# A fused adaLN / spectral mixer / MLP forward and backward kernel: loads of the first stage in a stated order, modulation rows dealt out singly, eight early blocks, and the first MLP block placed ahead of the last tile's products

## The chip, the core and the metric

The kernel runs on one core of a Trainium2 chip as a single launch. The metric is the device time of one execution in microseconds (us), from runs without the profiler; three runs of the kernel before are known, and their median is the number to beat. Separately, one execution was taken by the hardware profiler; every trace row in this document comes from such an execution. TensorE (PE) does the matrix products, VectorE (DVE) and ScalarE (ACT) do the elementwise work and empty PSUM, GpSimd (POOL) makes index tables and issues indirect transfers and many stores, and SyncE (SP) issues most loads. SP and POOL each issue in their own fixed order: an issue that waits holds up every issue behind it on that engine.

## The reference: what is computed

The reference is the forward pass of one block and its gradient (a VJP) for one sequence of 2048 tokens with 1024 features. Cut to what matters:

```python
def _A_ref(x, w_r, w_i):                  # spectral mixer
    X = rfft2(x) ; X = X * (w_r + 1j * w_i)
    return irfft2(X)
def _B_ref(x, w1, b1, w2, b2):            # MLP, 1024 -> 3584 -> 1024
    return gelu(layernorm(x) @ w1 + b1) @ w2 + b2
sa, ca, ga, sb, cb, gb = split6(silu(c) @ w_mod)
h = layernorm(x) * (1 + ca) + sa ;  x = x + ga * _A_ref(h)
h = layernorm(x) * (1 + cb) + sb ;  x = x + gb * _B_ref(h)
out, vjp = jax.vjp(...) ;  returns out and vjp(grad_out) for nine inputs
```

Arrays are bf16. The six rows `sa` to `gb` are rows 0 to 5 of the modulation.

## The kernel before

**Stages.** Both transforms are written as products with cosine and sine matrices. PE goes through these stages: modulation rows and a transposition of `grad_out`; the product `gb*grad_out` times `w2` transposed, called `pp` and stored as `d_ph`, which the gradient of the GELU needs later; the forward spectral mixer; more of `pp`; the MLP forward in four token blocks (`z_block` for the first matrix, `bo_pass` for the second); and from about 700 us on the backward stages and weight gradients, which no line of the change touches.

**How the order comes about.** The program is traced in Python; a scheduler then puts the instructions of each engine into a fixed order, earlier traced work first where it can run, later traced work in the gaps it expects. `tc.issue_after(ins)` keeps the instructions of a block behind `ins` on the engine of `ins` alone, and `behind(a, b)` does so for one pair. `ordered()` means: behind the last matrix product that was noted in `last_pe`. A tile with a tag takes over the memory of an earlier tile with that tag once that one's last reader is done.

**First stage (L264 to L395).** `mod_block(r, h)` (L272) makes half `h` of modulation row `r`: eight products of a 1 MB weight block `wblk` into a PSUM buffer of the two in `ps_s`, and one copy out of it. The blocks go round a ring of three tiles (`mod_tile`, L264), so that a load waits for the products three blocks before. Rows 1 and 5 come first. `load_tok` (L141) loads a quarter of the tokens: one 512 KB transfer from SP and two indirect ones from POOL. `load_go` (L349) loads a 1 MB quarter of `grad_out`; L381 to L395 transpose the four quarters on PE, four 128x128 products for each of 32 PSUM tiles (four buffers, `ps_f`), and DVE and ACT alternately scale each tile by `gb_col` into `gBoT0` to `gBoT3`. `gb_col` comes from both halves of row 5. `load_w2t(fg)` (L340) loads two chunks (256 rows) of `w2` with a transposing DMA into one of two halves of `wt`.

**The early `pp` chunks (L802 to L827).** `ph_part(fc, js)` makes chunk `fc` (of 28) for the token quarters `js`: eight products for each quarter into a `ps_f` buffer, and a copy out on ACT or DVE; I call one such quarter a part. `PH_EARLY = 6` chunks are traced ahead of the layer norms and folds that feed the spectral mixer (L829 to L846); the scheduler pulls later chunks forward as filler. Behind the products of chunk 3 stand three modulation blocks in a row, and behind chunk 5 three more (rows 2, 3 and 4). Row 0 and the table generator `gen_mats` are traced ahead of all `pp`.

**The late chunks and the first MLP block (L882 to L1055).** `load_w2t(fc // 2)` is issued as the two chunks before in the same half of `wt` are done. `load_w1` puts the seven 1 MB tiles of `w1` on SP behind given `w2` loads: two at chunk 22, one at chunk 24, four at chunk 26. The last four chunks get only quarters 0 and 1 at first. Then comes a list, `plan` (L1030): MLP block (0, 0), quarters 2 and 3 of chunks 24 to 27, MLP blocks (0, 1) and so on. `z_block` (L918) loads `n3T` (the normed tokens, transposed), makes four groups of eight products into `ps_s` and `ps_d`, and copies them to `zb`, a tile over the memory of `gBoT0` and `gBoT1`.

Of the kernel before, what the change touches and what calls it, by code (L numbers as in the profile page):

```python
# [10 lines left out]
FP32 = mybir.dt.float32  # L11
BF16 = mybir.dt.bfloat16
# [5 lines left out]
P = 128  # L18
# [17 lines left out]
def kernel(  # L36
# [104 lines left out]
    def load_tok(t4, src, i, eng=None):  # L141
        s3 = tok_flat(src)
        ins = (eng or nc.sync).dma_start(out=tok_plain(t4, i), in_=tok_rows(s3, i, 0, D))
# [120 lines left out]
    def mod_tile():  # L264
        wring[0] += 1
        return reg.tile([P, NDC, KH], BF16, name="wblk", tag=PXT[3 + wring[0] % 3])

    def mod_load(r, h, wblk, eng):
        cb = 2 * r + h
        eng.dma_start(out=wblk, in_=w_mod[:, cb * KH:(cb + 1) * KH].rearrange("(j p) n -> p j n", p=P))  # L270

    def mod_block(r, h, wblk=None):  # L272
        if wblk is None:
# [66 lines left out]
    def load_w2t(fg):  # L340
        w2t_in[0] = nc.sync.dma_start_transpose(out=wt[:, fg % 2], in_=B_w2[fg * 256:(fg + 1) * 256, :])
        w2ts.append(w2t_in[0])
# [4 lines left out]
           fbuf[:, 2], fbuf[:, 3]]  # L347

    def load_go(j):  # L349
        nc.sync.dma_start(out=gos[j], in_=go_f[j * BW:(j + 1) * BW, :].rearrange("(a p) d -> p a d", p=P))  # L350

    wm = {}

    def mod_get(r, h):
        wm[r, h] = mod_tile()
        mod_load(r, h, wm[r, h][:], nc.sync)

    mod_get(1, 0)
    load_tok(x4s[0], A_x, 0)
    mod_get(1, 1)  # L360
    mod_get(5, 0)
    for h in range(2):
        mod_block(1, h, wm[1, h][:])
    mod_get(5, 1)
    load_go(0)
    load_w2t(0)
    load_go(1)
    load_tok(x4s[1], A_x, 1)
    load_go(2)
    load_go(3)  # L370
    for h in range(2):
        mod_block(5, h, wm[5, h][:])
    load_tok(x4s[2], A_x, 2)
    load_tok(x4s[3], A_x, 3)
    load_w2t(1)
    pc = ps_d("pc")
    for cch in range(NDC):
        nc.tensor.matmul(pc[:, cch:cch + 1], lhsT=gb_row[0:1, cch * P:(cch + 1) * P], rhs=ones_bf[0:1, 0:1], start=True, stop=True)
# [398 lines left out]
        nc.vector.tensor_copy(out=out, in_=in_)  # L777


    for h in range(2):  # L780
        mod_block(0, h)
    gen_mats()
    gb2s = small.tile([P, NDC], FP32, tag="u_rt", bufs=1)
    nc.vector.reduce_sum(out=gb2s[:], in_=gu[:, 0:4, :].rearrange("p j c -> p c j"), axis=AX.X)
    gb2_bf = small.tile([P, NDC], BF16, tag="gc_bf", bufs=1)
    nc.vector.tensor_copy(out=gb2_bf[:], in_=gb2s[:])
    to_rows(gb2r, gb2_bf[:], NDC, ident[:])
    nc.gpsimd.dma_start(out=out_7.rearrange("(c p) -> c p", p=P), in_=gb2r)
    nc.gpsimd.dma_start(out=b1r, in_=B_b1.rearrange("(f p) -> f p", p=P))
    to_cols(b1_col[:], b1r, NFC, ident[:])  # L790
    nc.vector.tensor_scalar(out=sar[:, 0], in0=sar[:, 0], scalar1=8.0, scalar2=None, op0=ALU.mult)
    fold_d(saf.rearrange("p (c d) -> p c d", c=1), sar[:, 0], sar[:, 1])


    pho = reg.tile([P, 3, 4, BW], BF16, name="pho", tag="ot")
    phs = [pho[:, k] for k in range(3)] + [reg.tile([P, 4, BW], BF16, name="phr", tag="ph")[:]]
    last_pe = [None]

    def ordered():
# [118 lines left out]
    def z_block(b, g0, g1):  # L918
        n3T = n3Ts[b % 2]
        if g0 == 0:  # L920
            with tc.issue_after(w2ts[11].ins) if b == 0 else ExitStack():
                n3_in = nc.sync.dma_start_transpose(out=n3T[:], in_=d_n3[b * BW:(b + 1) * BW, :])
            if b == 0:
                for ins in w1_in[:2]:
                    behind(ins, n3_in)
        for g in range(g0, g1):
            n = b * 7 + g
            zb, av, bv, sg, ph = gts[n % 2]
            hh = hh_slots[n % 11]
            with tc.issue_after(w2t_in[0].ins) if n < 2 else ExitStack():  # L930
                nc.sync.dma_start(out=ph, in_=d_ph_v[:, g * 4:(g + 1) * 4, b * BW:(b + 1) * BW])
            for k in range(4):
                fc = g * 4 + k
                pz = (ps_s, ps_d)[k % 2]("pz")
                for cch in range(NDC):
                    with ordered():
                        last_pe[0] = nc.tensor.matmul(pz[:], lhsT=w1s[g][:, cch, k * P:(k + 1) * P], rhs=n3T[:, cch, :],  # L937
                                                      start=(cch == 0), stop=(cch == NDC - 1))
                with tc.high_priority():
                    z_in = nc.scalar.activation(out=zb[:, k, :], in_=pz[:], func=ACT.Identity, bias=b1_col[:, fc:fc + 1], scale=1.0)  # L940
            if n == 3:
                behind(n3_sqrt, z_in)
            elif n == 4:
                for ins in n3_norm:
                    behind(ins, z_in)
            with after_ev():
                nc.scalar.activation(out=av, in_=zb, func=ACT.Square)  # L947
            nc.vector.tensor_scalar(out=av, in0=av, scalar1=GC, scalar2=1.0, op0=ALU.mult, op1=ALU.add)
            tt(bv, av, zb, ALU.mult)
            with after_ev():  # L950
                nc.scalar.activation(out=sg, in_=bv, func=ACT.Sigmoid, scale=2.0 * GK)  # L951
            with after_ev():
                nc.scalar.activation(out=bv, in_=bv, func=ACT.Sigmoid, scale=-2.0 * GK)  # L953
            nc.vector.tensor_scalar(out=av, in0=av, scalar1=6.0 * GK, scalar2=-4.0 * GK, op0=ALU.mult, op1=ALU.add)
            tt(hh, sg, zb, ALU.mult)
            nc.gpsimd.dma_start(out=d_hh_v[:, g * 4:(g + 1) * 4, b * BW:(b + 1) * BW], in_=hh)
            tt(av, av, bv, ALU.mult)
            tt(av, av, hh, ALU.mult)
            tt(av, av, sg, ALU.add)
            if b < 2:  # L960
                tt(ph, ph, av, ALU.mult)
            for k in range(4 if b >= 2 else 0):
# [588 lines left out]
```

## Time and profile before

| what | value |
|---|---|
| runs without profiler | 1415.97, 1416.61, 1421.49 us; median 1416.61 us |
| the profiled execution, its own time | 1419.22 us |
| its span, first to last instruction | 1417.4 us |
| mean granted TensorE clock | 0.990 |
| DMA | 333.22 MB, mean 235 GB/s |

The profiled execution spends 1.8 us outside its span. Busy shares are read with care: a product is counted from its start to a modelled end, so "busy" PE rows hold some pipeline, and a few per cent of the product records are missing. In timeline rows the first column is the start, the second the length of a merged run of instructions, `x` the recorded number, and the bracket the idle time of that engine just before, with what ended it. In rows by stretches, each engine has its busy time and in brackets the number of instructions; then come the granted TensorE clock, the share of DMA time, and GB/s.

### The profile page before, as it was taken

The numbers are of one execution on the slowest core, as the hardware profiler recorded it, in microseconds if no ns is written. First come the engines' busy times: TensorE is split into PE (matmuls) and PEld (weight loads), VectorE is DVE, ScalarE is ACT, GpSimd is POOL, SyncE is SP. The second block draws the span as 40 slices with busy tenths as digits, with TensorE's granted clock in tenths as the row PEclk, the third lists the DMA queues.
The fourth block names the chain that finished last, engine by engine and source line by source line (L and its number), as shares of the span: only waits on it lengthen the run. The fifth ranks groups of instructions, "written<-read, shape, count | busy, mean of one in ns | idle before, by whom it ended". The sixth has DMA issues, their size and how long they took to land. (4 is left out here: it accounts for less than half of the span.)

```text
span 1417.4 us, 18569 instructions
## 1 busy us (share of the span) xinstructions
PE 1367.5 (96%) x6839; PEld 663.0 (47%) x6963; DVE 1071.1 (76%) x1503; ACT 745.6 (53%) x1063; POOL 377.1 (27%) x479
## 2 busy tenths in 40 slices
PE   5999999999999999999999999999999999999998
PEld 2545675444444444444444444344544565444443
DVE  5898889987698877886520788999488659898642
ACT  4775667667887765666315583343623445343211
POOL 5500623201112122212210011011367432322332
PEclk8899999999999999999999999999999999999999
DMA  9972647899688776687999399996699997666993
GB/s 330 304 226 72 181 137 226 261 277 348 239 235 267 231 252 233 200 275 232 292 287 233 115 271 319 210 298 193 191 279 281 242 242 207 189 180 182 288 261 118
DMA packets 356689, 333.22 MB, mean 235 GB/s; under 512 B 207578, under 2 KB 297200, under 8 KB 356470
## 3 DMA queue, kind: packets, MB, share of 16 engines
q1 hardware_dynamic: 319110, 205.61, 55.1%
q0 software_dynamic: 37488, 126.42, 25.7%
q8 instruction: 54, 0.88, 0.3%
q14 instruction: 37, 0.30, 0.1%
HBM read 166.77 MB, written 115.92 MB: 199 GB/s over the span
## 5 line engine op out<-in xcount | busy, mean ns | idle before, releaser
L808 PE MATMUL pp<-gBoT,wt 128*128 128x512 bf16 x874 | 196.3, 381 | 4.0 <-DMA wt<-in_B_w_dram 2.8
L1094 PE MATMUL pg<-w1T,gzr 128*128 128x512 bf16 x877 | 195.0, 379 | 3.7 <-ACT gn3b L1109 1.7
L1445 PE MATMUL gw1acc<-gzh,n3n 128*128 128x512 bf16 x877 | 194.1, 379 | 1.0
L1094 PEld LDWEIGHTS <-gzr 128*128 128x128 bf16 x896 | 86.4, 98 | 110.8 <-issue 7.9
L808 PEld LDWEIGHTS <-wt 128*128 128x128 bf16 x896 | 87.6, 98 | 107.5 <-DMA wt<-in_B_w_dram 3.3
L937 PEld LDWEIGHTS <-w 128*128 128x128 bf16 x896 | 87.1, 98 | 107.4 <-issue 2.7
L1445 PEld LDWEIGHTS <-n3n 128*128 128x128 bf16 x896 | 87.2, 98 | 105.2 <-issue 1.3
L937 PE MATMUL pz<-n3Ta,w 128*128 128x512 bf16 x439 | 98.2, 379 | 1.8 <-ACT gt L940 1.3
L937 PE MATMUL pz<-n3Tb,w 128*128 128x512 bf16 x436 | 98.0, 379 | 0.7 <-issue 0.2
L940 ACT ACTIVATE gt<-pz,b_col 128x512 bf16<-128x512 f32 x112 | 73.5, 684 | 38.1 <-PE pz L937 37.6
L994 PEld LDWEIGHTS <-hhA 128*128 128x128 bf16 x608 | 58.9, 98 | 73.4 <-issue 3.0
L1227 PE MATMUL gw2acc<-gB,hhsA 128*128 128x512 bf16 x406 | 91.2, 379 | 0.5
L1449 ACT CAST gwo<-gw1acc 128x512 bf16<-128x512 f32 x49 | 28.5, 582 | 111.0 <-PE gw1acc L1445 103.2
L194 DVE TENSOR_TENSOR gt<-gt,gt 128x2048 bf16<-128x2048 bf16 x56 | 68.5, 1224 | 20.6 <-ACT gt L953 19.4
L951 ACT ACTIVATE gt<-gt 128x2048 bf16<-128x2048 bf16 x28 | 53.5, 1910 | 55.1 <-DVE gt L194 55.1
L194 DVE TENSOR_TENSOR ct<-ct 128x2048 bf16<-128x2048 bf16 x68 | 80.8, 1217 | 1.4 <-DMA d_n<-ct 0.5
L1234 ACT CAST gwo<-gw2acc 128x512 bf16<-128x512 f32 x46 | 26.7, 582 | 101.0 <-PE gw2acc L1227 83.2
L1227 PEld LDWEIGHTS <-hhsA 128*128 128x128 bf16 x416 | 40.6, 98 | 47.9
L947 ACT ACTIVATE gt<-gt 128x2048 bf16<-128x2048 bf16 x28 | 53.5, 1910 | 1.7 <-DVE w2sA L194 1.0
L1450 POOL DMA_DIRECT2D out_dram<-gwo x56 | 30.7, 549 | 88.6 <-ACT gwo L1449 66.2
L953 ACT ACTIVATE gt<-gt 128x2048 bf16<-128x2048 bf16 x28 | 53.4, 1908 | 0.4
L814 ACT CAST pho<-pp 128x512 bf16<-128x512 f32 x59 | 33.5, 582 | 32.4 <-PE pp L808 31.9
(346 smaller groups left out, 2544.5 us busy)
## 6 DMA issues: line engine op xcount, KB each, us to landing
gzr<-d_gz SPq DMA_DIRECT2D x28, 512.0 KB, 6.4
wblk<-in_w_mod_dram SPq DMA_DIRECT2D x12, 1024.0 KB, 8.8
out_dram<-otl POOLq DMA_DIRECT2D x48, 256.0 KB, 4.5
out_dram<-gwo POOLq DMA_DIRECT2D x96, 128.0 KB, 4.2
d_ph<-pho POOLq DMA_DIRECT2D x21, 512.0 KB, 5.6
d_hh<-hhA POOLq DMA_DIRECT2D x19, 512.0 KB, 5.0
w<-in_B_w_dram SPq DMA_DIRECT2D x7, 1024.0 KB, 11.7
hhC<-d_ph SPq DMA_DIRECT2D x14, 512.0 KB, 9.5
```

The source lines that it names most:

```text
L194: return nc.vector.tensor_tensor(out=out, in0=a, in1=b, op=op)
L808: last_pe[0] = nc.tensor.matmul(pp[:], lhsT=wt[:, fg % 2, cch, k * P:(k + 1) * P], rhs=gBoT[j][:, cch, :], start=(cch == 0), stop=(cch == ...
L814: nc.any.tensor_copy(out=ov, in_=pv)
L937: last_pe[0] = nc.tensor.matmul(pz[:], lhsT=w1s[g][:, cch, k * P:(k + 1) * P], rhs=n3T[:, cch, :], start=(cch == 0), stop=(cch == NDC - 1))
L940: z_in = nc.scalar.activation(out=zb[:, k, :], in_=pz[:], func=ACT.Identity, bias=b1_col[:, fc:fc + 1], scale=1.0)
L947: nc.scalar.activation(out=av, in_=zb, func=ACT.Square)
L951: nc.scalar.activation(out=sg, in_=bv, func=ACT.Sigmoid, scale=2.0 * GK)
L953: nc.scalar.activation(out=bv, in_=bv, func=ACT.Sigmoid, scale=-2.0 * GK)
L994: last_pe[0] = nc.tensor.matmul(pbs[i][:], lhsT=hh[:, k, i * P:(i + 1) * P], rhs=wp[:, k, :], start=False, stop=(g == 6 and k == 3))
L1094: last_pg[0] = nc.tensor.matmul(pgs[i][:], lhsT=gzs[b, g][:, k, i * P:(i + 1) * P], rhs=w1Ts[g][:, k, h * KH:(h + 1) * KH], start=(g == 0 ...
L1227: nc.tensor.matmul(acc[:], lhsT=hh_of(fc)[:, t, :], rhs=gBs[t // 4][:, t % 4, h * KH:(h + 1) * KH], start=(t == 0), stop=(t == NT - 1))
L1445: nc.tensor.matmul(acc[:], lhsT=n3ns[t // 4][:, t % 4, cch * P:(cch + 1) * P], rhs=gz2[t // 8][:, t % 8, :], start=(t == 0), stop=(t == NT ...
```

## The change

Four things are edited.

1. The loads of the first stage are chained on SP with `start_load`: row 1 half 0, token quarter 0, row 1 half 1, row 5 half 0, `grad_out` quarter 0; then row 5 half 1, `grad_out` quarters 1, 2 and 3, token quarter 1, `w2` tile 0, token quarters 2 and 3, `w2` tile 1. Only SP instructions are chained; the indirect loads on POOL are not.
2. Chunks 0 and 1 of `pp` are traced ahead of row 0 and `gen_mats`, and row 0's products stand behind chunk 1's.
3. `PH_EARLY` is 8. The six late modulation blocks are put singly behind given parts (`MOD_AT`), two or three parts apart.
4. Chunks 26 and 27, quarters 0 and 1, move behind MLP block (0, 0) in `plan` (kind "q"). `w1` tiles are loaded one at chunk 22, one at chunk 24, five at chunk 26, and the last five stand behind the first load of `d_ph`.

```diff
     def mod_load(r, h, wblk, eng):
...
+        return eng.dma_start(out=wblk, in_=w_mod[:, cb * KH:(cb + 1) * KH].rearrange("(j p) n -> p j n", p=P))
...
-    mod_get(1, 0)
-    load_tok(x4s[0], A_x, 0)
-    mod_get(1, 1)
-    mod_get(5, 0)
+    last_ld = [None]
+
+    def start_load(what, *a):
+        with tc.issue_after(last_ld[0].ins) if last_ld[0] else ExitStack():
+            if what == "w":
+                wm[a] = mod_tile()
+                last_ld[0] = mod_load(*a, wm[a][:], nc.sync)
+            elif what == "t":
+                load_w2t(*a)
+                last_ld[0] = w2t_in[0]
+            elif what == "g":
+                last_ld[0] = load_go(*a)
+            else:
+                last_ld[0] = load_tok(x4s[a[0]], A_x, a[0])
+
+    for what in (("w", 1, 0), ("x", 0), ("w", 1, 1), ("w", 5, 0), ("g", 0)):
+        start_load(*what)
     for h in range(2):
         mod_block(1, h, wm[1, h][:])
-    mod_get(5, 1)
-    load_go(0)
-    load_w2t(0)
-    load_go(1)
-    load_tok(x4s[1], A_x, 1)
-    load_go(2)
-    load_go(3)
+    for what in (("w", 5, 1), ("g", 1), ("g", 2), ("g", 3), ("x", 1), ("t", 0), ("x", 2), ("x", 3), ("t", 1)):
+        start_load(*what)
     for h in range(2):
         mod_block(5, h, wm[5, h][:])
-    load_tok(x4s[2], A_x, 2)
-    load_tok(x4s[3], A_x, 3)
-    load_w2t(1)
...
-    phs = [pho[:, k] for k in range(3)] + [reg.tile([P, 4, BW], BF16, name="phr", tag="ph")[:]]
+    phs = [pho[:, k] for k in range(3)]
...
-    PH_EARLY = 6
+    for fc in range(2):
+        ph_part(fc, (0, 1, 2, 3))
+    with ordered():
+        for h in range(2):
+            mod_block(0, h)
+    gen_mats()
...
+    phs.append(reg.tile([P, 4, BW], BF16, name="phr", tag="ph")[:])
+
+    PH_EARLY = 8
+    MOD_AT = ((3, 3), (4, 1), (4, 3), (5, 2), (6, 0), (6, 2))
     late_mods = [(r, h) for r in (2, 3, 4) for h in range(2)]
-    for fc in range(PH_EARLY):
-        ph_part(fc, (0, 1, 2, 3))
-        if fc % 2 == 1:
-            load_w2t(fc // 2 + 2)
-            if fc > 1:
-                with tc.issue_after(last_pe[0].ins):
-                    for r, h in late_mods[3 * (fc // 2 - 1):3 * (fc // 2)]:
-                        mod_block(r, h)
+    load_w2t(2)
+    for fc in range(2, PH_EARLY):
+        for j in range(4):
+            ph_part(fc, (j,))
+            if j == 3 and fc % 2 == 1:
+                load_w2t(fc // 2 + 2)
+            if (fc, j) in MOD_AT:
+                with ordered():
+                    mod_block(*late_mods[MOD_AT.index((fc, j))])
...
-            load_w1((0, 2, 1, 4)[max(fc // 2 - 10, 0)])
-        ph_part(fc, (0, 1, 2, 3) if fc < PH_KEEP else (0, 1))
+            load_w1((0, 1, 1, 5)[max(fc // 2 - 10, 0)])
+        if fc < NFC - 2:
+            ph_part(fc, (0, 1, 2, 3) if fc < PH_KEEP else (0, 1))
...
-                for ins in w1_in[:2]:
-                    behind(ins, n3_in)
+                behind(w1_in[0], n3_in)
...
+                ph_in = nc.sync.dma_start(out=ph, in_=d_ph_v[:, g * 4:(g + 1) * 4, b * BW:(b + 1) * BW])
+            for ins in w1_in[2:] if n == 0 else ():
+                behind(ins, ph_in)
...
-    plan = [("z", 0, 0)] + [("p", fc, 0) for fc in range(PH_KEEP, NFC)] + [("z", 0, 1), ("z", 0, 2), ("z", 0, 3)]
+    plan = [("z", 0, 0)] + [("q", fc, 0) for fc in range(NFC - 2, NFC)] + [("p", fc, 0) for fc in range(PH_KEEP, NFC)] + [("z", 0, 1), ("z", 0, 2), ("z", 0, 3)]
...
+        elif kind == "q":
+            with ordered():
+                ph_part(b, (0, 1))
```

More of the change, by code (lines that the diff above doesn't have):

```diff
@@ L269, in mod_load @@
         cb = 2 * r + h
-        eng.dma_start(out=wblk, in_=w_mod[:, cb * KH:(cb + 1) * KH].rearrange("(j p) n -> p j n", p=P))
+        return eng.dma_start(out=wblk, in_=w_mod[:, cb * KH:(cb + 1) * KH].rearrange("(j p) n -> p j n", p=P))
     def mod_block(r, h, wblk=None):
@@ L349, in load_go @@
     def load_go(j):
-        nc.sync.dma_start(out=gos[j], in_=go_f[j * BW:(j + 1) * BW, :].rearrange("(a p) d -> p a d", p=P))
+        return nc.sync.dma_start(out=gos[j], in_=go_f[j * BW:(j + 1) * BW, :].rearrange("(a p) d -> p a d", p=P))
     wm = {}
-    def mod_get(r, h):
-        wm[r, h] = mod_tile()
-        mod_load(r, h, wm[r, h][:], nc.sync)
-    mod_get(1, 0)
-    load_tok(x4s[0], A_x, 0)
-    mod_get(1, 1)
-    mod_get(5, 0)
+    last_ld = [None]
[13 more added lines that the diff above has]
+        start_load(*what)
     for h in range(2):
         mod_block(1, h, wm[1, h][:])
-    mod_get(5, 1)
-    load_go(0)
-    load_w2t(0)
-    load_go(1)
-    load_tok(x4s[1], A_x, 1)
-    load_go(2)
-    load_go(3)
+    for what in (("w", 5, 1), ("g", 1), ("g", 2), ("g", 3), ("x", 1), ("t", 0), ("x", 2), ("x", 3), ("t", 1)):
+        start_load(*what)
     for h in range(2):
         mod_block(5, h, wm[5, h][:])
-    load_tok(x4s[2], A_x, 2)
-    load_tok(x4s[3], A_x, 3)
-    load_w2t(1)
     pc = ps_d("pc")
@@ L777, in dve_copy @@
         nc.vector.tensor_copy(out=out, in_=in_)
[L780 to L792, printed above, removed]
     pho = reg.tile([P, 3, 4, BW], BF16, name="pho", tag="ot")
-    phs = [pho[:, k] for k in range(3)] + [reg.tile([P, 4, BW], BF16, name="phr", tag="ph")[:]]
+    phs = [pho[:, k] for k in range(3)]
     last_pe = [None]
@@ L816, in ph_part @@
             nc.gpsimd.dma_start(out=d_ph[fc * P:(fc + 1) * P, :], in_=ph2.rearrange("p i w -> p (i w)"))
-    PH_EARLY = 6
-    late_mods = [(r, h) for r in (2, 3, 4) for h in range(2)]
-    for fc in range(PH_EARLY):
-        ph_part(fc, (0, 1, 2, 3))
-        if fc % 2 == 1:
-            load_w2t(fc // 2 + 2)
-            if fc > 1:
-                with tc.issue_after(last_pe[0].ins):
-                    for r, h in late_mods[3 * (fc // 2 - 1):3 * (fc // 2)]:
-                        mod_block(r, h)
+    for fc in range(2):
[4 more added lines that the diff above has]
+    gen_mats()
+    gb2s = small.tile([P, NDC], FP32, tag="u_rt", bufs=1)
+    nc.vector.reduce_sum(out=gb2s[:], in_=gu[:, 0:4, :].rearrange("p j c -> p c j"), axis=AX.X)
+    gb2_bf = small.tile([P, NDC], BF16, tag="gc_bf", bufs=1)
+    nc.vector.tensor_copy(out=gb2_bf[:], in_=gb2s[:])
+    to_rows(gb2r, gb2_bf[:], NDC, ident[:])
+    nc.gpsimd.dma_start(out=out_7.rearrange("(c p) -> c p", p=P), in_=gb2r)
+    nc.gpsimd.dma_start(out=b1r, in_=B_b1.rearrange("(f p) -> f p", p=P))
+    to_cols(b1_col[:], b1r, NFC, ident[:])
+    nc.vector.tensor_scalar(out=sar[:, 0], in0=sar[:, 0], scalar1=8.0, scalar2=None, op0=ALU.mult)
+    fold_d(saf.rearrange("p (c d) -> p c d", c=1), sar[:, 0], sar[:, 1])
+    phs.append(reg.tile([P, 4, BW], BF16, name="phr", tag="ph")[:])
+    PH_EARLY = 8
+    MOD_AT = ((3, 3), (4, 1), (4, 3), (5, 2), (6, 0), (6, 2))
+    late_mods = [(r, h) for r in (2, 3, 4) for h in range(2)]
+    load_w2t(2)
[7 more added lines that the diff above has]
+                    mod_block(*late_mods[MOD_AT.index((fc, j))])
     for i in range(4):
@@ L930, in z_block @@
             with tc.issue_after(w2t_in[0].ins) if n < 2 else ExitStack():
-                nc.sync.dma_start(out=ph, in_=d_ph_v[:, g * 4:(g + 1) * 4, b * BW:(b + 1) * BW])
+                ph_in = nc.sync.dma_start(out=ph, in_=d_ph_v[:, g * 4:(g + 1) * 4, b * BW:(b + 1) * BW])
+            for ins in w1_in[2:] if n == 0 else ():
+                behind(ins, ph_in)
             for k in range(4):
```

## The prediction

> **What bounds the kernel now.** I read the page's shares first, then the view of waits for PE up to 130 us and from there to 350 us, then PE's timeline wherever a wait stands, then SP's timeline for what it waits for. The share row and the two views of waits:
>
> ```profile
> PE 1367.5 (96%) x6839; PEld 663.0 (47%) x6963; DVE 1071.1 (76%) x1503; ACT 745.6 (53%) x1063; POOL 377.1 (27%) x479
> ...
> PE pm L278 <- DMA wblk<-in_w_mod_dram: 10.8, 4, 5.1
> ...
> PE pm L278 <- ACT rows L281: 1.9, 1, 1.9
> PE pm L278 <- DVE sb_saf L281: 1.4, 1, 1.4
> ...
> PE pu L535 <- DVE fbuf L194: 1.3, 1, 1.3
> ...
> PE pp L808 <- DMA wt<-in_B_w_dram: 2.8, 1, 2.8
> ```
>
> PE is busy for 1367.5 of 1417.4 us, so it sets the end: what the change can win is PE's idle time and the time in which its clock is down, no more than about 50 us in all, and no product is removed. The columns of the wait rows are the total, the number of waits and the longest. The change touches these waits and no other: the first stage, the two at the modulation copies, the one at `wt`. PE's timeline of the first stage, and stretches of it with all engines:
>
> ```profile
> 18.17 3.59 PE L278 MATMUL pm<-wblk,u_b 128*128 128x512 bf16 x8 [5.12 <-DMA wblk<-in_w_mod_dram]
> ...
> 24.15 1.90 PE L278 MATMUL pm<-wblk,u_b 128*128 128x512 bf16 x7 [0.57 <-DMA wblk<-in_w_mod_dram]
> ...
> 28.14 0.40 PE L386 MATMUL pt<-ident,go 128*128 128x128 bf16 x4 [1.06 <-DVE gBoT L390]
> ...
> 31.06 3.76 PE L386 MATMUL pt<-ident,go 128*128 128x128 bf16 x32 [1.20 <-DMA go<-in_grad_out_dram]
> 37.26 4.19 PE L386 MATMUL pt<-ident,fbuf 128*128 128x128 bf16 x36 [2.43 <-DMA fbuf<-in_grad_out_dram]
> 41.72 2.68 PE L386 MATMUL pt<-ident,fbuf 128*128 128x128 bf16 x28 [0.27 <-ACT gBoT L394]
> 44.43 3.83 PE L808 MATMUL pp<-gBoT,wt 128*128 128x512 bf16 x16
> ```
>
> ```profile
> 24.00:28.00 4.00, 2.09 (x11) 0.86 (x12) 2.11 (x9) 3.89 (x5) 3.14 (x5) 1.00 1.00 253
> ...
> 32.00:36.00 4.00, 2.81 (x25) 2.38 (x23) 3.55 (x10) 3.79 (x8) 0.00 (x0) 0.50 1.04 399
> 36.00:40.00 4.00, 2.73 (x24) 2.57 (x25) 2.14 (x6) 1.82 (x7) 0.00 (x0) 0.50 1.05 394
> ```
>
> The DMA is full (shares of 1.00 to 1.05) all the way; the `pp` products, of which there is then no lack, begin at 44.43 us. They begin so late because all 128 transposing products stand ahead of them, and those wait for `grad_out` quarters 1 (until 31.06) and 2 (until 37.26).
>
> **Part 1, the order of the first loads.** The issues of SP in that time, and the groups that scale the transposed tiles (busy time, mean ns of one, idle before):
>
> ```profile
> 11.13 12.82 SPq L341 DMA_TRANSPOSE wt<-in_B_w_dram  x1
> 24.01 0.57 SPq L350 DMA_DIRECT2D go<-in_grad_out_dram  x1
> 24.62 0.51 SPq L143 DMA_DIRECT2D x<-in_A_x_dram  x1
> 25.17 1.74 SPq L350 DMA_DIRECT2D fbuf<-in_grad_out_dram  x2
> ...
> L390 DVE TENSOR_SCALAR_CACHE_REDUCE gBoT<-pt,gb_col 128x512 bf16<-128x512 f32 x16 | 11.8, 749 | 4.2 <-PE pt L386 3.6
> L394 ACT ACTIVATE gBoT<-pt,gb_col 128x512 bf16<-128x512 f32 x16 | 10.8, 681 | 3.9 <-PE pt L386 3.5
> L394 ACT ACTIVATION_READ_ACCUMULATOR gBoT<-pt,gb_col 128x1 f32 x16 | 3.1, 196 | 0.0
> ```
>
> The transposing load of `w2` tile 0 held SP for 12.82 us, until the queue ahead of it had drained, and the next `grad_out` quarter was issued only then, at 24.01. After the change three quarters stand ahead of it. Up to the row 5 block that PE got at 24.15 the sequence on SP is the one that it was already, so `gb_col` comes no earlier. Behind it, at the rate of 394 to 399 GB/s that plain loads show, a 1 MB (1.05 million byte) quarter takes 2.7 us: quarters 1, 2, 3 land at about 26.9, 29.6 and 32.3, token quarter 1 at 33.6, `w2` tile 0 at 35.7 if at the 253 GB/s of the stretch in which it was moved before, and I put 37, with the stores of tables between. Then what is late next is the scaling: it starts near 28, has 16 tiles on each engine, and ACT's tile costs 0.68 + 0.20 = 0.88 us, so 28 of the 32 take 14 x 0.88 = 12.3 us before the last four can go: the transposition ends at 40.5, or about 41 with some of the sines and norms that share the engines. Gain 44.4 - 41 = 3.5 us. Bounds: 0, if `w2` tile 0 comes as late as `pp` begins now, and 5.5, with 0.75 us (DVE's tile) instead of 0.88 and nothing between. `w2` tile 1, now last of 14, is wanted two chunks (some 14 us) after that and costs nothing. Row 0, now behind chunk 1, keeps its 16 products; they were beside other products already.
>
> **Part 2, the modulation blocks dealt out.** PE's timeline around the two rows of three:
>
> ```profile
> 76.14 3.62 PE L278 MATMUL pm<-wblk,u_b 128*128 128x512 bf16 x15
> 81.64 1.89 PE L278 MATMUL pm<-wblk,u_b 128*128 128x512 bf16 x8 [1.89 <-ACT rows L281]
> ...
> 97.17 3.62 PE L278 MATMUL pm<-wblk,u_b 128*128 128x512 bf16 x16
> 102.17 1.89 PE L278 MATMUL pm<-wblk,u_b 128*128 128x512 bf16 x7 [1.38 <-DVE sb_saf L281]
> ```
>
> Two blocks fill both buffers of `ps_s`, the third waits for the first copy: 1.89 + 1.38 = 3.27 us of idle PE, with work at hand. Two blocks take 3.62, one 1.8; a part of eight products takes 13.98/8 = 1.75 us (64 products, 62 recorded, in the row at 331.75 below). With at least two parts between blocks, a buffer is asked for again two blocks later, after 2 x (2 x 1.75 + 1.8) = 10.6 us, when the longest lag seen is 1.89 + 1.8 = 3.7. Gain 3.3; bounds 0 (a wait of the same size elsewhere) and 3.3. The copies and the loads are as many as before. Two chunks more ahead of the folds put up to eight copies of some 0.7 us on DVE ahead of them; the wait of 1.3 us at the folds can so vanish or grow, and PE has products of the next chunks to fill it: I cost it at nothing, between -1.3 and +3.
>
> **Part 3, the last tiles.** PE's timeline around the wait, then SP's:
>
> ```profile
> 224.81 81.75 PE L808 MATMUL pp<-gBoT,wt 128*128 128x512 bf16 x371
> 309.33 15.68 PE L808 MATMUL pp<-gBoT,wt 128*128 128x512 bf16 x62 [2.77 <-DMA wt<-in_B_w_dram]
> 324.84 7.07 PE L937 MATMUL pz<-n3Ta,w 128*128 128x512 bf16 x32
> 331.75 13.98 PE L808 MATMUL pp<-gBoT,wt 128*128 128x512 bf16 x62
> ...
> 281.87 4.38 SPq L922 DMA_TRANSPOSE n3Ta<-d_n  x1
> 286.43 0.46 SPq L879 DMA_DIRECT2D w<-in_B_w_dram  x1
> ...
> 290.08 0.90 SPq L879 DMA_DIRECT2D w<-in_B_w_dram  x1
> 292.77 8.78 SPq L341 DMA_TRANSPOSE wt<-in_B_w_dram  x1
> 301.66 0.85 SPq L879 DMA_DIRECT2D w<-in_B_w_dram  x1
> 306.58 5.59 SPq L341 DMA_TRANSPOSE wt<-in_B_w_dram  x1
> ```
>
> Behind the wait come 64 products, chunks 24 to 27 by halves; so the tile waited for is that of chunks 24 and 25, issued at 292.77 with two `w1` tiles just ahead of it, and not the last one, issued at 306.58. The change takes one of those two away, 2.7 us at the best rate seen above and 4.1 at 253 GB/s, against a wait of 2.77. The wait goes, just. The last tile has 13.8 us and more from its issue until chunk 26 now, since MLP block (0, 0) stands between. That block needs `n3T` and one `w1` tile, both issued 20 us ahead; its copy waits for chunk 27 to be done with `gBoT0`, and its four buffers are not those of `pp`. The wait has a second price: the same 64 products take 15.68 us right behind it and 13.98 later. Gain 2.77 + 1.70 = 4.5, between 0 (both late) and 4.5. A rule speaks against the second half: the Trainium skill's page "TensorE: Matmul & The Clock Gate" (Part 1, the HAM clock gate) lets the clock fall only after an idle window of about 3.4 us, so that a gap of 2.77 might cost nothing more. By that the gain would be 2.8 and the sum below 1.7 smaller; the two rows disagree with it, and I follow them.
>
> **The sum.** 3.5 + 3.3 + 4.5 = 11.3 us off PE's path. Against it I put one new wait of the size of the folds' 1.3, since four orders change at once and each engine's order is fixed: 10.0 us. The profiled execution took 1419.2 and would take 1409.2; it lies 2.6 above the median of the plain runs, 1416.6, so the number to compare is 1406.6, say 1407. Behind 350 us all is shifted alike.
>
> **Rivals.** (a) The start stays: `w2` tile 0, three quarters later than it was, lands no earlier than the transposition ends now. For it: the 12.82 us that its issue took behind a full queue; against it, the bytes ahead are fewer than those that land by 40 now. It leaves 3.3 + 4.5 - 1.3: 1410. (b) The first 6.8 us are given back: the folds on DVE end when they did, PE has spent its filler early and stands idle in the mixer. For it, DVE without a pause in the stretch below (9.97 of 10 us); against it, 371 products of filler that come after 224.81 in one piece. It leaves 4.5: 1412.
>
> ```profile
> 100.00:110.00 10.00, 8.51 (x40) 3.84 (x40) 9.97 (x11) 6.28 (x9) 0.00 (x0) 1.00 0.29 81
> ...
> 65.16 13.23 SPq L341 DMA_TRANSPOSE wt<-in_B_w_dram  x2
> ...
> DMA to landing us min/median/max: 8.8/8.8/10.6
> ```
>
> (c) Slower: the pinned modulation blocks wait for their weights. Each load behind the third goes into the tile that a block frees three blocks earlier, seven parts and two blocks, 7 x 1.75 + 2 x 1.8 = 15.9 us, before its own place; the last row, of the line that loads them, gives 8.8 to 10.6 us to land. It decides when SP holds the load for more than 5.3 us, as it held two `w2` tiles for 13.23. PE cannot step past a block in its order. Three such loads, each at the longest wait seen for such a block, 5.12, and each followed by eight products at 3.59 instead of 1.89: 3 x 6.8 = 20.4, less 11.3: 9 slower, 1426.
>
> **Chances.** The forecast 0.48, (a) 0.14, (b) 0.17, (c) 0.21. A measurement of this kernel tells about 0.5%, 7.1 us, from no change, so faster means under 1409.5 and slower over 1423.7. The forecast is nearly all faster (0.44 of 0.48); (a) lies on the line, and I count 0.04 of it as faster; (b) is the same; of (c) half is past the line and half is not, with one or two late loads only, and 0.05 of the rest goes to slower for a wait that no row shows: 0.48, 0.36, 0.16. The forecast's own range is 1403 (no new wait, start at its better bound) to 1411. For 8 in 10 the range takes in (a), (b) and one or two late loads of (c), each 6.8, with the early gains gone: 1401 to 1422.
>
> **What would show it.** Part 1: the first `pp` product at 40 to 42 us, `grad_out` quarters 1 to 3 issued ahead of any transposing load; wrong if PE waits for `wt` there. Part 2: no wait at L278 for L281 past 50 us; wrong if a wait for `wblk` or a new wait at the folds stands in its place. Part 3: no wait for `wt` near 300 us, 7 us of `pz` ahead of the last 32 products of the first halves, and a clock of 1.00 there. The whole is wrong if PE's idle time up to 350 us falls by less than 5 us, or if the mixer's stretches hold new waits for DVE.

## The result, and the profile after

| | before | changed |
|---|---|---|
| median of 22 runs each | 1419.20 us (1414.71 to 1423.31) | 1422.47 us (1418.43 to 1427.93) |
| ratio to before, 95% interval | | 1.0025 [1.0014, 1.0037] |
| span of the profiled execution | 1417.4 us | 1420.2 us |
| mean granted clock | 0.990 | 0.994 |

The changed kernel is 0.25% slower, 3.5 us; forecast were 10.0 us less. The share row of its page, and the group of the `pp` products (busy, mean ns, idle before; the line is L794 now, it was L808):

```profile
PE 1378.0 (97%) x6963; PEld 662.5 (47%) x6963; DVE 1069.6 (75%) x1499; ACT 747.6 (53%) x1067; POOL 373.3 (26%) x479
...
L794 PE MATMUL pp<-gBoT,wt 128*128 128x512 bf16 x896 | 203.1, 385 | 6.0 <-DVE phr L800 2.3
```

The idle time ahead of `pp`, 4.0 us before and 2.8 of it the wait for `wt` that was to go, is 6.0 us, and copies out of PSUM end 4.0 of it (2.3 on DVE and 1.7 on ACT). The view of waits of PE, up to 130 us and then to 350 us (total, number, longest):

```profile
PE pm L278 <- DMA wblk<-in_w_mod_dram: 9.3, 4, 4.1
PE ptr L209 <- DVE sar L281: 2.9, 1, 2.9
PE pu L536 <- DVE fbuf L194: 2.2, 1, 2.2
...
PE pp L794 <- DVE phr L800: 2.3, 2, 1.5
PE pp L794 <- DMA wt<-in_B_w_dram: 2.1, 1, 2.1
PE pp L794 <- ACT phr L800: 1.7, 1, 1.7
```

Each wait that the change was aimed at is gone: `pm` for a copy of `rows` (1.9), `pm` for `sb_saf` (1.4), `wt` at 309 us (2.8). Four others have come, and the one at the folds has grown from 1.3 to 2.2. PE's timeline places them:

```profile
39.24 13.98 PE L794 MATMUL pp<-gBoT,wt 128*128 128x512 bf16 x64
53.05 3.62 PE L278 MATMUL pm<-wblk,u_b 128*128 128x512 bf16 x16
59.53 0.27 PE L209 MATMUL ptr<-ident,gb_bf 128*8 128x128 bf16 x1 [2.86 <-DVE sar L281]
...
81.72 1.89 PE L278 MATMUL pm<-wblk,u_b 128*128 128x512 bf16 x8
...
119.26 0.83 PE L536 MATMUL pu<-smA,fbuf 128*128 128x256 bf16 x6 [2.20 <-DVE fbuf L194]
...
280.52 29.49 PE L794 MATMUL pp<-gBoT,wt 128*128 128x512 bf16 x128 [2.05 <-DMA wt<-in_B_w_dram]
311.66 1.89 PE L794 MATMUL pp<-gBoT,wt 128*128 128x512 bf16 x8 [1.66 <-ACT phr L800]
315.02 5.34 PE L794 MATMUL pp<-gBoT,wt 128*128 128x512 bf16 x24 [1.48 <-DVE phr L800]
320.20 7.07 PE L947 MATMUL pz<-n3Ta,w 128*128 128x512 bf16 x32
```

`pp` begins 5.2 us sooner (39.24 for 44.43). Row 0's two blocks now fill both buffers of `ps_s`, and the transposition of `gb2` behind them, the third user in a row, waits 2.86 us for row 0's copy. What the change took apart in the late rows, two blocks in a row in front of a third user, has come back at a new place. The mixer's products then wait longer for the folds, and between 280 and 340 us stand a tile of weights that was never late before (chunk 20's) and waits for copies. All of it adds up: the group of MLP products that began at 345.56 begins at 348.82, 3.3 us later, and from there to the end this distance changes by no more than 0.5 us.

What is late first in that last stretch is on SP and POOL. SP's timeline before and after (a row marked `x2` is two transposing loads merged, from the start of the first to the end of the second):

```profile
265.15 16.62 SPq L341 DMA_TRANSPOSE wt<-in_B_w_dram  x2
...
289.65 0.38 SPq L865 DMA_DIRECT2D d_n<-ct  x1
```

```profile
264.69 19.39 SPq L341 DMA_TRANSPOSE wt<-in_B_w_dram  x2
284.16 8.30 SPq L931 DMA_TRANSPOSE n3Ta<-d_n  x1
292.56 0.94 SPq L873 DMA_DIRECT2D d_n<-ct  x1
```

and POOL's, before and after:

```profile
264.92 0.72 POOL L143 DMA_DIRECT2D xt<-in_A_x_dram  x1 [0.64 <-ACT ct L512]
266.51 2.92 POOL L145 DMA_INDIRECT xt<-in_A_x_dram,xu  x1 [0.87 <-ACT ct L512]
269.44 0.79 POOL L854 DMA_DIRECT2D d_A<-ct  x1
```

```profile
264.61 0.74 POOL L143 DMA_DIRECT2D xt<-in_A_x_dram  x1 [0.57 <-ACT ct L513]
265.34 0.78 POOL L862 DMA_DIRECT2D d_A<-ct  x1
266.43 1.67 POOL L145 DMA_INDIRECT xt<-in_A_x_dram,xu  x1 [0.30 <-ACT pho L800]
```

The `x2` rows are the loads of two `wt` tiles. Both kernels issue the first, for chunks 20 and 21, at 265 us; the second, for chunks 22 and 23, goes out 13.8 us later in every kernel here, when PE is done with the other half of `wt`, and it is then that PE wants chunk 20's weights. SP issues nothing in between. In the changed kernel the store of the mixer's output (`d_A`, 1 MB) stands ahead of the last gather of token rows and goes out 0.65 us behind that load instead of 4.29; a second store, `d_x`, stands ahead of two gathers 25 us earlier. No line of the change touches these stores: the scheduler, which places POOL's instructions by the times it expects, has swapped them. The trace's records of single DMA packets show the first tile (2048 packets of 256 bytes, 0.52 MB) through 14.8 us after its issue, for 5.8 before: between 272 and 279.5 us SP's queue moved 0.13 MB and POOL's, which carries `d_A`, 1.9 MB. So PE waits 2.05 us for it. The second tile's load holds SP for 5.57 us instead of 2.81, `n3Ta`'s for 8.30 instead of 4.38, so the store of the normed tokens (`d_n`) goes out 2.9 us later. DVE waits for it, and ACT, whose copies PE needs, waits for DVE:

```profile
300.03 1.23 DVE L194 TENSOR_TENSOR ct<-ct 128x2048 bf16<-128x2048 bf16 x1 [5.82 <-DMA d_n<-ct]
...
310.84 0.30 ACT L478 ACTIVATE mv<-mv,eps_c 128x4 f32<-128x4 f32 x1 [7.12 <-DVE mv L489]
```

Before, DVE's wait was 0.46 us and ACT's 4.77. The copies of `pp` stand behind such work on DVE and ACT, in a fixed order. Where the granted clock fell, by stretches of the changed kernel (after the engines: clock, DMA share, GB/s):

```profile
60.00:70.00 10.00, 10.00 (x35) 3.83 (x34) 8.19 (x23) 4.98 (x8) 3.10 (x4) 0.72 0.97 326
...
120.00:130.00 10.00, 9.98 (x69) 7.33 (x68) 4.71 (x6) 6.69 (x12) 0.00 (x0) 0.83 0.00 0
280.00:290.00 10.00, 9.48 (x37) 3.99 (x38) 6.06 (x16) 9.55 (x14) 0.54 (x1) 0.83 1.20 230
```

Three of the waits are followed by a lower clock; 128 products took 29.49 us behind the one at 280 where two undisturbed sets of 64 take 27.96.

### The profile page after: what moved, and what is told of

The parts are those of the page before. It is cut to its first block, busy times and chain, and to the rows that moved or that the text cites. A ratio compares the mean times of both kernels' runs of the same rounds, so it can differ in the third digit from the quotient of the medians.

```text
span 1420.2 us, 18707 instructions
## 1 busy us (share of the span) xinstructions
PE 1378.0 (97%) x6963; PEld 662.5 (47%) x6963; DVE 1069.6 (75%) x1499; ACT 747.6 (53%) x1067; POOL 373.3 (26%) x479
## 5 line engine op out<-in xcount | busy, mean ns | idle before, releaser
L794 PE MATMUL pp<-gBoT,wt 128*128 128x512 bf16 x896 | 203.1, 385 | 6.0 <-DVE phr L800 2.3
L794 PEld LDWEIGHTS <-wt 128*128 128x128 bf16 x896 | 88.4, 99 | 115.2 <-issue 13.4
```

What stands on the lines that cost most here:

```text
L794: last_pe[0] = nc.tensor.matmul(pp[:], lhsT=wt[:, fg % 2, cch, k * P:(k + 1) * P], rhs=gBoT[j][:, cch, :], start=(cch == 0), stop=(cch == ...
```

## The experiments

Twelve kernels, each in five rounds against the kernel before. Beside the ratio with its 95% interval stand three readings of each trace: where the mixer's products begin behind their wait for the folds, where `pp` restarts behind the mixer, and DVE's wait for block 1's `d_n` store to land, with the time at which DVE goes on.

| kernel | ratio to before | mixer | `pp` again | DVE for `d_n` |
|---|---|---|---|---|
| before | | 122.16 | 220.27 | 0.46, 297.68 |
| changed | 1.0025 [1.0014, 1.0037] | 119.26 | 219.81 | 5.82, 300.03 |
| e1: changed, late part undone | 1.0018 [1.0002, 1.0033] | 116.77 | 216.04 | 6.10, 296.33 |
| e2: before, late part alone | 0.9989 [0.9976, 1.0002] | 121.56 | 219.71 | none, 296.67 |
| e6: before, order of first loads alone | 0.9996 [0.9978, 1.0015] | 118.02 | 216.00 | 4.68, 297.84 |
| e7: changed, first loads as before | 0.9991 [0.9980, 1.0003] | 121.04 | 220.42 | 0.28, 298.22 |
| e3: changed, `gb2` in another pool | 1.0015 [1.0005, 1.0025] | 117.08 | 218.25 | 4.16, 296.59 |
| e8: e3, early copies on ACT | 1.0008 [0.9989, 1.0028] | 115.08 | 214.44 | 4.92, 296.52 |
| e5: changed, both stores in their old places | 0.9957 [0.9938, 0.9976] | 118.62 | 219.29 | none, 293.60 |
| e9: changed, `d_A` alone in its old place | 0.9970 [0.9960, 0.9981] | 117.98 | 217.08 | none, 291.38 |
| e11: e3 and e5 together | 0.9974 [0.9963, 0.9985] | 117.16 | 218.34 | none, 292.66 |
| e12: e11, nine early chunks | 1.0011 [0.9996, 1.0025] | 116.75 | 217.19 | 7.14, 295.70 |
| e10: e2, both stores moved ahead | 1.0011 [0.9991, 1.0031] | 121.93 | 219.82 | 1.06, 298.05 |

The twelfth, e4 (1.0085 [1.0064, 1.0107]), moves the `d_n` store itself. The last column sorts the kernels: every one that is clearly below the kernel before (e5, e9, e11) has no wait there. The front does begin the mixer sooner, by 1.1 to 7 us, and part of that reaches the restart of `pp`; where DVE then waits 4 us or more for `d_n`, it goes on at 296 to 300 us, at most 2.0 us sooner than the kernel before (297.68). One profile places a wait, and the ratio weighs it: the changed kernel, e5 and e9 have the same orders on every engine up to 230 us, and yet `pp` restarts at 219.81, 219.29 and 217.08.

**Which part loses (e1, e2, e6, e7).** e1 is the changed kernel without its fourth edit, e2 the kernel before with that edit alone:

```diff
-            load_w1((0, 2, 1, 4)[max(fc // 2 - 10, 0)])
-        ph_part(fc, (0, 1, 2, 3) if fc < PH_KEEP else (0, 1))
+            load_w1((0, 1, 1, 5)[max(fc // 2 - 10, 0)])
+        if fc < NFC - 2:
+            ph_part(fc, (0, 1, 2, 3) if fc < PH_KEEP else (0, 1))
...
-    plan = [("z", 0, 0)] + [("p", fc, 0) ...
+    plan = [("z", 0, 0)] + [("q", fc, 0) for fc in range(NFC - 2, NFC)] + [("p", fc, 0) ...
```

> The changed kernel with its late part undone: w1's loads, the phases and the products behind the last w2 tile are as in the kernel before, and the start and the modulation blocks as changed. Theory: DVE's folds set when the mixer begins, so the front gives back nearly all of its gain (the products behind the mixer began 0.46 us earlier), and the loss comes from the late part; this kernel then takes 0.999 to 1.001 of the kernel before, and chunk 20's products wait no 2.05 us for their weights. Rival: the stalls of 280 to 340 us come from the front, whose shift moved stores and loads on the queues; then this kernel takes 1.002 or more of the kernel before, and the waits of 2.05, 1.66 and 1.48 us are there.

> The kernel before with the late part alone. Theory: the late part costs some 3 us; 1.002 to 1.003 of the kernel before, with waits of products for their weights or for the copies of their sums between 280 and 340 us. Rival: the front made those stalls, and the late part alone gains what its removed wait cost (2.8 us) or nothing; 0.997 to 1.000.

My theory of that hour, that the late part costs and the front only gives its gain back, is wrong in both. The late part alone comes out 1.6 us lower (e2, with an interval that just takes in no change), the front alone 2.6 higher (e1). The late `wt` is in e1 (2.16 us at 276.64) and not in e2, where of the late stretch this is left:

```profile
311.66 1.89 PE L808 MATMUL pp<-gBoT,wt 128*128 128x512 bf16 x8 [0.49 <-DVE phr L814]
313.39 7.07 PE L939 MATMUL pz<-n3Ta,w 128*128 128x512 bf16 x31
...
332.18 10.52 PE L808 MATMUL pp<-gBoT,wt 128*128 128x512 bf16 x47 [1.36 <-DVE phr L814]
```

The wait of 2.77 us and the slow products behind it are gone; 1.85 us come back as waits for copies.

e6 puts the chain of first loads into the kernel before, and e7 takes it out of the changed one:

```diff
-    mod_get(1, 0)
-    load_tok(x4s[0], A_x, 0)
...
+    for what in (("w", 5, 1), ("g", 1), ("g", 2), ("g", 3), ("x", 1), ("t", 0), ("x", 2), ("x", 3), ("t", 1)):
+        start_load(*what)
```

> The kernel before with the order of the first loads alone (Part 1). Theory: the products begin about 5 us sooner, the three late blocks behind one another still wait 1.89 and 1.38 us, and the fold wait of 1.26 us grows by 3 us or more, since a fixed number of products lies ahead of it; the mixer starts 1 to 2 us sooner at most and the time is 0.998 to 1.001 of the kernel before. Rival, PE sets the pace: the fold wait stays under 2 us and the time is 0.996 to 0.997.

> The changed kernel with the first loads in the order of before (Parts 2 and 3 alone). Its stores on POOL stand in the order of the kernel before. Theory: no late wt at 280 us; the wait of 2.86 us behind chunk 1 is there, the fold wait is that of before or less (under 2.2 us), and the time is 0.997 to 1.000 of the kernel before. Rival: dealing out the modulation blocks and the eight early blocks cost by themselves; 1.001 or more.

Neither can be told from the kernel before. In e6 the fold wait hardly grew (1.32 us), against what I expected: the start's gain passes the folds, and `pp` restarts 4.3 us sooner. By the timeline it is lost at `d_n`, for which DVE waits 4.68 us to go on at 297.84, where it went on before (297.68); no run takes that wait out of e6. In e7 POOL's two stores stand where they stood before, in e6 `d_A` is moved ahead of the last gather; so it is the order of the first loads that makes the scheduler swap it.

**Does a gain ahead of the folds last (e3, e8, e12)?** e3 takes away the wait of 2.86 us:

```diff
...
-    to_rows(gb2r, gb2_bf[:], NDC, ident[:])
+    to_rows(gb2r, gb2_bf[:], NDC, ident[:], ps_d)
...
-    to_cols(b1_col[:], b1r, NFC, ident[:])
+    to_cols(b1_col[:], b1r, NFC, ident[:], ps_d)
```

> The changed kernel, with the transpositions of gb2 and of b1 behind chunk 1 put into a buffer of another pool, so that they are not the third user in a row of a pool of two buffers. Both theories: the wait of 2.86 us at 59.5 us goes, and the clock of 0.72 in 60 to 70 us comes up. Theory that PE's products set the pace: 5 us less than the changed kernel, 0.9985 of the kernel before. Rival, that DVE's folds set when the mixer begins and a fixed number of products lies ahead of it: the wait for the folds grows from 2.2 to 6 us or more, the products behind the mixer begin at 219 to 220 us as they did, and the time is that of the changed kernel, 1.002 to 1.003.

PE's timeline of e1, which has the changed kernel's front with the wait (but a clock of 1.00 from 60 to 70 us, where the changed kernel had 0.72), and of e3:

```profile
59.27 0.22 PE L209 MATMUL ptr<-ident,gb_bf 128*8 128x128 bf16 x1 [2.86 <-DVE sar L281]
...
116.77 0.83 PE L536 MATMUL pu<-smA,fbuf 128*128 128x256 bf16 x6 [2.23 <-DVE fbuf L194]
```

```profile
56.69 0.22 PE L209 MATMUL ptr<-ident,gb_bf 128*8 128x128 bf16 x1
...
108.98 2.32 PE L794 MATMUL pp<-gBoT,wt 128*128 128x512 bf16 x10
117.08 1.46 PE L536 MATMUL pu<-smA,fbuf 128*128 128x256 bf16 x6 [5.78 <-DVE fbuf L194]
```

PE is 2.6 us ahead at 57 us, and the mixer begins at 117.08 for 116.77. In these two executions all that the edit won has turned into wait for the folds (5.78 for 2.23). The stretches of e3 say who holds it (the third engine is DVE):

```profile
90.00:100.00 10.00, 9.95 (x47) 4.56 (x47) 10.00 (x13) 5.38 (x8) 0.53 (x1) 1.00 0.72 219
100.00:110.00 10.00, 9.95 (x48) 4.62 (x48) 9.93 (x10) 5.34 (x10) 0.69 (x2) 1.00 0.21 81
110.00:117.00 7.00, 1.30 (x7) 0.39 (x4) 6.90 (x9) 0.58 (x1) 0.37 (x1) 0.82 0.59 150
```

DVE is without a gap; PE has 266 `pp` products ahead of the mixer in its order, whether it reaches their end early or late. The rival that DVE sets the mixer's start holds for this part of the gain; in the whole e3 is 1.4 us below the changed kernel, within both intervals. e8 takes copies off DVE:

```diff
-                nc.any.tensor_copy(out=ov, in_=pv)
+                if 3 <= fc < 8:
+                    nc.scalar.copy(out=ov, in_=pv)
+                else:
+                    nc.any.tensor_copy(out=ov, in_=pv)
```

> As e3 (the transpositions in a buffer of the other pool), with the copies of chunks 3 to 7 put on ACT by hand; in e3 DVE does about 11 of the early copies, 8 us, and has no gap between 84 and 117 us. Theory, DVE's folds set when the mixer begins: the folds end 3 to 7 us sooner (e3: 117.1), the mixer's products begin as much sooner, and the wait for the folds falls under 3 us (e3: 5.78). Rival: DVE waits for ACT's norms in turn, so that the copies only move; the folds end within 1.5 us of e3's 117.1. For the whole time: up to 4 us less than e3 by the first, the same by the rival.

The mixer began 2.0 us sooner than in e3, less than the least that the theory asked for (3), and PE still waited 5.84 us, with ten products fewer ahead of it. It shows the direction and no more; the 3.8 us by which `pp` restarts sooner than in e3 are gone at `d_n` (DVE goes on at 296.52, in e3 at 296.59). e12 fills the wait instead:

```diff
-    PH_EARLY = 8
+    PH_EARLY = 9
```

> e11 with nine chunks of w2^T products ahead of the mixer in place of eight, 32 products where about 12 stood: some 20 more products (4.3 us) in front of the mixer's, meant to fill the fold wait of 5.8 us. Theory: that wait falls to under 2 us and what it held is gained, up to 4 us below e11 (0.991 to 0.995 of the kernel before), unless the other orders that are set anew (POOL's again) take it back: then the waits behind 220 us grow and it is no better than e11.

The fold wait fell to 1.16 us, as meant, and e12 is 0.37% slower than e11. The newly made orders brought other waits later, PE's below and DVE's 7.14 us for `d_n` in the table, though both pins stand and chunk 20's tile was through 6.2 us after its issue: a late tile is not the only thing that brings that wait.

```profile
299.82 7.08 PE L796 MATMUL pp<-gBoT,wt 128*128 128x512 bf16 x32 [1.31 <-DMA wt<-in_B_w_dram]
323.55 6.81 PE L796 MATMUL pp<-gBoT,wt 128*128 128x512 bf16 x23 [2.84 <-DVE pho L802]
...
389.19 1.21 PE L954 MATMUL pz<-n3Ta,w 128*128 128x512 bf16 x3 [2.77 <-ACT gt L957]
```

**The order on POOL (e4, e5, e9, e10, e11).** e4 was a try at the middle of the chain, the `d_n` store behind SP's transposing load:

```diff
-        nc.sync.dma_start(out=chunk_rows(d_n3, i), in_=tmp)
+        nc.gpsimd.dma_start(out=chunk_rows(d_n3, i), in_=tmp)
```

> The changed kernel, with the stores of the third norm's result issued on POOL's queue in place of SP's. Theory: block 1's store was ready at 286.6 us and went out at 292.56 since SP was held by a transposing load issued at 284.16, which made DVE wait 5.82 us at 300, and the copies behind it held up the products (1.66, 1.48 and 0.83 us); then DVE's wait falls under 1 us, those waits shrink to under 1 us together, and the time falls by 3 to 4 us against the changed kernel, to 0.999 to 1.000 of the kernel before. Rival: the copies stand behind the norms on ACT and DVE whichever queue the store takes; the waits of products stay at 3 us or more, and the time is that of the changed kernel, 1.002 to 1.003.

It missed: chunk 20's products waited 15.43 us for their weights, the load of the next tile held SP until 295 us, and the kernel lost 8.5 us against the changed one. A store moved to another queue is a new order on both. e5 therefore leaves every queue its own and pins the two stores to their places of before; e9 pins `d_A` alone:

```diff
-        nc.gpsimd.dma_start(out=chunk_rows(d_A, i), in_=o4)
+        a_in = nc.gpsimd.dma_start(out=chunk_rows(d_A, i), in_=o4)
         load_tok(x4, A_x, i, nc.gpsimd)
+        if i in (2, 3):
+            behind((x1_in, A_in)[i - 2][0], gather_in[0])
+        A_in[0] = a_in
...
```

> The changed kernel, with two stores on POOL's queue pinned to their places of before: block 1's d_x behind both gathers of block 2's rows, and block 2's d_A behind the last gather of block 3's rows. All other orders are those of the changed kernel. Theory: with the front the two stores moved ahead of the gathers, the transposing load of chunk 20's weights took 19.39 us beside them instead of 16.62, and the wait of 2.05 us, the late store of the norm and the waits for copies of 1.66 and 1.48 us all follow; then that load takes about 16.6 us again, the waits between 280 and 320 us fall under 1.5 us together, and the kernel takes 0.998 to 1.000 of the kernel before. Rival: DVE's and ACT's own order makes them; the load may be quicker but the waits stay, and the time is that of the changed kernel, 1.002 to 1.003.

> As e5, with block 2's d_A alone pinned behind the last gather; d_x stays ahead of the gathers as in the changed kernel. If the d_A store beside the transposing load of chunk 20's weights makes the load late: as e5, load of 16.3 us, no wait at 280 us, 0.995 to 0.998 of the kernel before. If it is the d_x store of 239 us, or both are needed: the load takes over 18 us, the wait of some 2 us at 280 is there, 1.001 to 1.003.

Both expectations, and e10's below, call the whole `x2` row (19.39 us in the changed kernel, 16.62 before) the load of chunk 20's weights. In e5 these two swaps are all that differs from the changed kernel's orders, in e9 the one. SP's, POOL's and PE's timelines of e9:

```profile
261.95 15.65 SPq L343 DMA_TRANSPOSE wt<-in_B_w_dram  x2
277.69 5.31 SPq L938 DMA_TRANSPOSE n3Ta<-d_n  x1
283.90 0.40 SPq L880 DMA_DIRECT2D d_n<-ct  x1
```

```profile
263.46 1.89 POOL L147 DMA_INDIRECT xt<-in_A_x_dram,xu  x1 [0.85 <-ACT ct L515]
265.35 0.80 POOL L866 DMA_DIRECT2D d_A<-ct  x1
```

```profile
269.74 35.34 PE L796 MATMUL pp<-gBoT,wt 128*128 128x512 bf16 x163
306.38 5.34 PE L796 MATMUL pp<-gBoT,wt 128*128 128x512 bf16 x24 [1.30 <-DVE phr L802]
```

`d_A` goes out 3.40 us behind the first load instead of 0.65 (the gather keeps its place, 1.51 for 1.74 us). The tile is through 6.7 us after its issue instead of 14.8, the `x2` row is 15.65 us long, the products of chunk 20 wait for nothing, `d_n` goes out 21.95 us behind the first load for 27.87, and of 6.02 us of waits between 280 and 340 us 2.13 are left (1.30 and 0.83). With the 1.5 us of clock (29.49 for 27.96) that is 5.4 of the 9.2 us between the two spans; 2.7 more were there at 217 us, ahead of the edit, and are no part of its effect. By the ratios, e9 takes 0.55% less than the changed kernel, 7.8 us, give or take 2.2 (the half widths 0.00115 and 0.00105 added in squares), and beats the kernel before by 0.3%, 4.3 us. e5 comes out 0.43% below the kernel before. One pin is enough. The pair e3 and e11, which differ by both pins, shows it again: 0.41%, 5.8 us, give or take 2.1.

The reverse, e10, moves both stores ahead in a kernel that has nothing of the front:

```diff
+        for ins in gather_in if i == 2 else ():
+            behind(ins, x1_in[0])
+        if i == 3:
+            behind(gather_in[1], A_in[0])
```

> The kernel before with the late part alone (e2, 0.9989 of the kernel before), with the two stores on POOL moved ahead of the gathers, as they stand in the changed kernel; nothing of the front. Theory, the order on POOL makes the loss: chunk 20's load takes over 18 us (e2: 16.64), its products wait about 2 us at 280, waits for copies of 3 us or more follow before 320 us, and the time is 1.001 to 1.003 of the kernel before. Rival, the order costs only behind the changed front: waits as in e2, 0.997 to 1.000.

The time is in the forecast place, 1.0011 for e2's 0.9989, but the intervals overlap, and a late tile was not the way: `d_A` went out 1.43 us behind the load, the tile was through after 5.6 us, and nothing waits at 280 us. Only the waits for copies grew, from 1.85 to 2.84 us. So the swap by itself does not make the tile late; how near the store comes to the load counts too. In e10 POOL waits 0.91 us at the store for DVE; in the changed kernel the store's data is there when its turn comes.

> e3 and e5 together: the transpositions in a buffer of the other pool and both stores pinned. If gains ahead of the mixer are lost at the fold wait: that wait is 5.8 us as in e3, the mixer starts 2 us sooner than in e5 (118.6), the time is within 2 us of e5's, 0.994 to 0.998. If the 5 us of e3 were only hidden by the late load: 3 to 5 us below e5, 0.991 to 0.993.

e11's fold wait is 5.77 us and its time that of e9: what e3 wins ahead of the mixer is lost again, with or without the late tile.

## Why the prediction was wrong

The steps from the kernel before to the changed one can be put in a row by three ratios: the late part alone (e2) -1.6 us, the front with `d_A` in its old place (e9 against e2) -2.7, `d_A` moved (changed against e9) +7.8, of which the timelines place 5.4; together +3.5. The prediction had -4.5, then -3.5 - 3.3 + 1.3 = -5.5, and nothing for the third. Each of these differences carries some 2 us of uncertainty, so that the first could be nothing and the second is only just clear of it.

- **The term that failed most** is the last of the sum: "Against it I put one new wait of the size of the folds' 1.3, since four orders change at once and each engine's order is fixed". It named the risk and priced it by a wait that already existed. What came was an order that no edit had touched, POOL's: a 1 MB store, now issued 0.65 us behind a load on SP, kept the last of that load's 0.52 MB back until 14.8 us after its issue (6.7 with the store put back), and that order cost 7.8 us where 1.3 stood for everything.
- **Part 1** was right in its place and too small: `pp` at 39.24, a gain of 5.2 within the bounds of 0 to 5.5, sooner than the 40 to 42 us named as the sign. That it would last to the end was not borne out: e6, which has this gain alone, holds 4.3 us of it at 216 us and takes 0.9996 of the kernel before, 0.6 us less with some 2.6 either way.
- **Part 2**: both waits, 3.27 us together, are gone, and no block waited for weights past 50 us, so rival (c) fell. But "Row 0, now behind chunk 1, keeps its 16 products; they were beside other products already" looked at the block's products and not at what uses the same two buffers next; 2.86 us came back there.
- **The folds**: "PE has products of the next chunks to fill it: I cost it at nothing, between -1.3 and +3" is the second step that failed, by its reason more than by its size. In the changed kernel the wait grew by 0.9 us, inside these bounds. But the filler is a fixed number of products, and it can be spent sooner than DVE is done: in e3, with the wait of 2.86 us out of the way, the fold wait of 5.78 is 4.5 above the old 1.3. Rival (b) had this mechanism with the folds ending when they did; they ended 2.9 us sooner in the changed kernel (119.26 for 122.16), so that it took a part of the front's gain only. The larger join, DVE's wait for `d_n`, was in no rival.
- **Part 3**: the wait for `wt` and the slow products behind it went as foreseen, in e2 with no other edit. The 4.5 us were mis-sized: 1.6 were left, give or take 1.8, and copies on DVE are what PE waits for next (1.85 us in all).
- "Behind 350 us all is shifted alike" held: 3.26 us at the second MLP group, 2.8 at the end.

Not settled: what part of the front's 2.7 us each of its edits brings, and why `d_n` is late in e6. Its tile of chunk 20 was in time (through after 11.3 us, wanted after 13.8) and the store went out at 285.59, but its last packet was through only 11.7 us later, where in the twelve other kernels with this store on SP it took 4.9 to 8.5. Two 1 MB tiles of `w1` stand around it on SP, issued 1.0 us ahead and 0.4 behind; no run shows whether they are the cause.

## What to carry to other kernels

Where a scheduler orders the queues, compare the instruction order of every engine before and after an edit, also of the queues that the edit does not touch: one store that goes past a gather can cost more than the edit wins. A gain of the busy engine can come back as a wait at the next join that a slower chain sets (here the folds, then the landing of a store), so find the joins behind an edit and what each of them waits for. When a block is moved, look at the next user of its buffers at the new place as well as at its own.

## What the runs showed of the hardware

**A store on one queue slowed a load on another.** By the packet records, the time from the issue of chunk 20's tile on SP to its last packet, by when POOL issued the 1 MB store `d_A`:

| `d_A` issued | tile through after |
|---|---|
| 2.26 us ahead of the load | 15.2 us (e8) |
| 0.30 us ahead | 11.3 us (e6) |
| 0.65 to 0.66 us behind | 14.8 us (changed), 14.6 (e1), 13.1 (e3) |
| 1.43 us behind | 5.6 us (e10) |
| 3.4 us behind | 7.3 us (e5), 6.7 (e9), 6.1 (e11) |
| 4.3 us or more behind | 5.8 us (before), 5.4 (e2), 6.2 (e7), 6.2 (e12) |

PE wants the tile 13.8 us after its issue, so PE does not wait for it in e6, and in e3 only 0.86 us. Where the turn lies between 0.66 and 1.43 us no run shows. The Trainium skill, page "DMA: Bandwidth & Descriptors", section "Rules for kernel authors", says that the DMAs of SP, ACT and GpSimd all run on the same 16 engines and interleave; these rows agree, and no run here shows what decides how the queues share them.

**The clock fell after gaps of 2 to 3 us, and not each time.** Behind gaps of 2.80 to 2.86 us at the same place, the stretch from 60 to 70 us had a clock of 0.72 (changed), 0.73 (e4), 0.83 (e5), 0.86 (e9) and 1.00 (e1); behind 2.05 us at 280, 0.83. The Trainium skill, page "TensorE: Matmul & The Clock Gate", Part 1 (the HAM clock gate), has the clock fall after at least one idle window of about 3.4 us and the window run freely; e1 agrees, in the others the clock fell after less. The step of the prediction that followed the rows of before instead (1.70 us behind a gap of 2.77) is borne out by them.
